# A fused linear-attention and two-layer kernel: dummy matmuls ahead of the first turning, the diagonals of two stages and the sums of three states moved off TensorE, and a redrawn head

## The chip, the cores and the metric

The kernel runs on one core of a Trainium2 chip. The metric is device microseconds (us) of one execution, the median of several runs. The core's engines each work through a stream of their own, in order: PE (TensorE, matmuls into the accumulators, eight banks called ps), DVE (VectorE), ACT (ScalarE), POOL (GpSimd, which here also issues the loads) and SP (which issues DMA transposes and the stores). Engines wait for each other on semaphores alone.

## What is computed

```python
state = zeros(B, H, D, D)                 # B, H, S, D = 4, 8, 768, 48
for t in range(S):
    cur = einsum('bhd,bhe->bhde', u * k[:, :, t], v[:, :, t])
    y[:, :, t] = einsum('bhd,bhde->bhe', r[:, :, t], state + cur)
    state = w[:, :, None] * state + einsum('bhd,bhe->bhde', k[:, :, t], v[:, :, t])
x = y.transpose(0, 2, 1, 3).reshape(3072, 384)
h = x @ w_in                              # 384 x 2048
out = maximum(0.01 * h, h) @ w_out        # 2048 x 384
```

Inputs and output are fp32; the kernel works in bf16 with fp32 accumulation.

## The kernel before

The 4 x 768 tokens are cut into 24 stages of 128 tokens, six to a batch element (`n % 6`). The recurrence is done stage by stage: inside a stage as a masked 128 x 128 product of decayed r and k, between stages by a state of 48 x 48 per head. Two stages make a pair `m` of 256 tokens for the two layers. Each step of a stage is a function, and a string of tokens, ORDER (L26 to L31), says in which order the steps of stages 0 to 9 are recorded; after it a loop (L725) does the rest pair by pair. Recording order is the order of each engine's stream, so a step that must wait holds up everything recorded behind it on the same engine. The tokens, with the number of the stage:

- `P` prep: DVE multiplies r and k by tables of decay (L322 and L324, from stage 8 on both in one, L315). From stage 8 (TURNED) SP then transposes the product by DMA (L317).
- `T` turn: for stages 0 to 7, PE transposes r and k by eight matmuls against `ident` (L367), and ACT copies the two banks out (L378; one of stage 0's on DVE, L375).
- `A`: eight matmuls give the 128 x 128 products (L391, two banks). `M`: DVE multiplies each bank by the triangular `mask` and writes `at` (L409), or from stage DIAG on overwrites only the part under the mask (L401), since `at` then already holds the diagonal.
- The diagonal (u) term. Below DIAG: `X`, a DVE product (L329), four matmuls with N = 2 inside `K` (L421), `Q`, a DVE product with v (L337), and three matmuls against `ident` inside `Y` (L513). From DIAG on: `Q` is three DVE instructions (L342, L344, L346) and two POOL tiles (L354).
- `K`: PE forms k-transposed times v (L425), and for stages below DIAG with `n % 6 > 0` adds the old state by one matmul against `ident` (L430). `S`: DVE multiplies by the decay (L475); from DIAG on it adds the old state itself first (L478, L480).
- `Y`: PE makes the stage's output (L508), ACT copies it to `xT` (L528). `G n.g`: 12 matmuls of layer one for one stage and a quarter of w_in (L541) and ACT's leaky ReLU (L546). `J m.j`: six matmuls for an eighth of w_in and a whole pair (L558). `H n`: layer two, 16 matmuls with N = 384 (L575). From pair 8 on layer two is done by seven half-size products (L639).
- `C` and `W`: 24 matmuls of one row (L449, L450), ACT's logarithms (L457) and tables (L466), DVE casts (L459) for the decays. `U`: one matmul and one copy for u's table (L710, L712). `F n`: n dummy matmuls, 128 x 512, of a tile of ones into the bank that is next (L254); nothing reads them. Three are there: two (EARLY) ahead of the broadcast of w (L294), one from the token `F1`.

Loads are issued by POOL (L217 a stage's r, k or v; L227 a quarter of w_in; L231 a quarter of w_out), stages 1 to 7 and all weights in the order of the string LOADS (L25), then the `L` tokens, which wait for a matmul of layer one (`pace`). POOL also makes `ident` (L262) and `mask` (L266) in the midst of the loads.

The eight banks are given out in rotation (`next_bank`): a step that takes a bank waits for whoever reads what was there eight takings ago.

Of the kernel before, what the change touches and what calls it, by code (L numbers as in the profile page):

```python
# [20 lines left out]
NFB = DFF // 128  # L21
NSL = HD // 128

FIRST, EARLY = 6, 2
LOADS = """r1 k1 r2 k2 wi0 id v1 r3 tri k3 v2 wi1 k4 r4 v3 wi2 k5 r5 r6 k6 v4 v5 k7 wi3 r7 v6 v7 wo3 wo2 wo1 wo0"""  # L25
ORDER = """  # L26
C W P0 P1 F1 T0 T1 P2 A0 X0 M0 A1 K0 T2 Q0 X1 Y0 A2 S0 M1 K1 X2 G0.0 Q1 P3 S1 Y1 T3 K2 M2 G1.0 X3 A3 U G0.1 S2 G1.1 Q2 M3 Y2 K3 P4
T4 Q3 G2.0 G2.1 G0.2 S3 G2.2 G1.2 Y3 P5 A4 P6 X4 M4 T5 X5 G3.0 K4 Q4 A5 S4 T6 G3.1 K5 G3.2 Y4 M5 L8 Q5 Y5 P7 A6 G1.3 J2.0 J2.1 T7
M6 X6 X7 K6 J2.2 J2.3 A7 S6 J2.4 J2.5 L9 Q6 G2.3 G0.3 J2.6 M7 L10 J2.7 L11 G3.3 K7 S7 P8 Q7 Q8 P9 H0 Q9 K8 H1 P10 L12 K9 H2 S8 S9
Y6 Y7 A8 A9 P11 M8 H3 M9 L13  # L30
"""  # L31


# [87 lines left out]
def bass_rwkv5_eagle__then__act_leaky_relu_kernel(  # L121
# [14 lines left out]
        return ctx.enter_context(nc.sbuf_tensor(name, shape, dt))  # L136

    NQK, NTP, NVS, NAT, NT, NX, NG, NO, NRK = 6, 6, 6, 6, 6, 3, 3, 4, 14
    TURNED, DIAG = 8, 8
    SEVEN = (8,9,10,11)  # L140
    HF, NH = NFB // 2, HD // 2
    w_in_sb = SB("w_in_sb", [128, NSL, DFF])
# [15 lines left out]
    tcol = SB("tcol", [128, 1], FP32)  # L158
# [7 lines left out]
    ones = SB("ones", [128, 512])  # L166
    mask = SB("mask", [128, 128])
    ident = SB("ident", [128, 128])
    ku = [SB(f"ku{i}", [128, HD]) for i in range(2)]
    rku = [SB(f"rku{i}", [128, HD]) for i in range(2)]  # L170
    s_tok = [SB(f"s_tok{i}", [128, H], FP32) for i in range(2)]
# [47 lines left out]
    def load_stage(n, pace=()):  # L219
        for which in "krv":  # L220
            load_one(n, which, pace)
# [12 lines left out]
    def row(h):  # L234
# [23 lines left out]

    ps_w, key_w = next_bank()

    def identity():
        add("pool", lambda: G.affine_select(ident[:, :], ones[:, 0:128], pattern=[[1, 128]], compare_op=ALU.is_equal,  # L262
                                            fill=0.0, base=0, channel_multiplier=-1), R=["ones"], W=["ident"])

    def triangle():
        add("pool", lambda: G.affine_select(mask[:, :], ones[:, 0:128], pattern=[[1, 128]], compare_op=ALU.is_ge,  # L266
                                            fill=0.0, base=-1, channel_multiplier=-1), R=["ones"], W=["mask"])

    for name in LOADS.split():
        if name == "id":  # L270
            identity()
        elif name == "tri":
            triangle()
        elif name[:2] == "wi":
            load_win(int(name[2:]))
        elif name[:2] == "wo":
            load_wout(int(name[2:]))
        else:
            load_one(int(name[1:]), name[0])

    add("dve", lambda: V.tensor_scalar(kexp[:, :], tcol[:, :], -1.0, float(MID - 1), ALU.mult, ALU.add),
        R=["tcol"], W=["kexp"])
    add("dve", lambda: V.tensor_scalar(qexp[:, :], tcol[:, :], 1.0, float(-MID), ALU.mult, ALU.add),
        R=["tcol"], W=["qexp"])
# [24 lines left out]

    def prep(n):  # L310
        iq = n % NQK
        if n >= TURNED:
            both = rk_sb[:, n % NRK, :, :].rearrange("p w (h d) -> p (w h) d", d=D)
            by = tab[:, :, :].rearrange("p w (h d) -> p (w h) d", d=D)
            add("dve", lambda: V.tensor_tensor(qk[iq][:, :, 0:D], both, by, ALU.mult),  # L315
                R=[("r", n % NRK), ("k", n % NRK), "qtab", "ktab", ("qk0", iq)], W=[("qp", iq), ("kp", iq)])
            add("sp", lambda: SP.dma_start_transpose(tp[n % NTP][:, :, :],  # L317
                                                     qk[iq][:, :, :].rearrange("p h e -> p (h e)")),
                R=[("kp", iq), ("qp", iq), ("qk0", iq)], W=[("tp", n % NTP, 0), ("tp", n % NTP, 1)],
                dma=f"tp{n % NTP}")  # L320
            return
        add("dve", lambda: V.tensor_tensor(qk[iq][:, 0:H, 0:D], hd(r_of(n)), hd(qtab[:, :]), ALU.mult),  # L322
            R=[("r", n % NRK), "qtab", ("qk0", iq)], W=[("qp", iq)])
        add("dve", lambda: V.tensor_tensor(qk[iq][:, H:2 * H, 0:D], hd(k_of(n)), hd(ktab[:, :]), ALU.mult),  # L324
            R=[("k", n % NRK), "ktab", ("qk0", iq)], W=[("kp", iq)])
# [33 lines left out]
    def turn(n):  # L359
        it, iq = n % NTP, n % NQK  # L360
        for half in ((0, 1) if n == 0 else (1, 0)):
            ps_t, key = next_bank()

            def emit(half=half, ps_t=ps_t):
                for p in range(NP):
                    h0 = half * H + 2 * p
                    last = PE.matmul(ps_t[:, 128 * p:128 * p + 128],  # L367
                                     qk[iq][:, h0:h0 + 2, :].rearrange("p h e -> p (h e)"), ident[:, :],
                                     start=True, stop=True)
                return last  # L370

            add("pe", emit, R=[("kp" if half else "qp", iq), ("qk0", iq), "ident"], W=[key])
            dst = tp[it][:, NP * half:NP * half + NP, :].rearrange("p m t -> p (m t)")
            if n == 0 and half == 1:
                add("dve", lambda dst=dst, ps_t=ps_t: V.tensor_copy(dst, ps_t[:, :]),  # L375
                    R=[key], W=[("tp", it, half)])
            else:
                add("act", lambda dst=dst, ps_t=ps_t: A.activation(dst, ps_t[:, :], AF.Copy),  # L378
                    R=[key], W=[("tp", it, half)])

    def a_mm(n):
        it = n % NTP
# [11 lines left out]

        add("pe", emit, R=[("tp", it, 0), ("tp", it, 1)], W=[key for _, key in at_bank[n]])

    def a_mask(n):
        if n >= DIAG:
            i = at_bank[n][0][1][1]
            halves = [("at", n % NAT, hh) for hh in range(2)]  # L400
            add("dve", lambda: V.copy_predicated(  # L401
                at[n % NAT][:, :, :, :].rearrange("p two m i -> p (two m) i"),
                mask[:, :].bitcast(mybir.dt.uint16).unsqueeze(1).to_broadcast([128, H, 128]),
                ps_all[:, 512 * i:512 * i + 1024].rearrange("p (m i) -> p m i", i=128)),
                R=[key for _, key in at_bank[n]] + ["mask"] + halves, W=halves)
            return
        for hh in range(2):
            part = at_bank[n][hh][0][:, :].rearrange("p (m i) -> p m i", i=128)
            add("dve", lambda hh=hh, part=part: V.tensor_tensor(  # L409
                at[n % NAT][:, hh, :, :], part, mask[:, :].unsqueeze(1).to_broadcast([128, NP, 128]), ALU.mult),  # L410
                R=[at_bank[n][hh][1], "mask"], W=[("at", n % NAT, hh)])

    def kv_mm(n):
        iq = n % NQK
        ps_kv, key = kv_bank[n] = next_bank()
        live, carried = n % NC < NC - 1, n < DIAG and n % NC > 0

        def emit():
            if n < DIAG:
# [288 lines left out]
    def u_table():  # L708
# [3 lines left out]
        add("act", lambda: A.activation(u_tab[:, :], ps_u[:, 0:HD], AF.Copy), R=[key], W=["u_tab"])  # L712

    steps = {"U": u_table, "P": prep, "Q": prep2, "T": turn, "A": a_mm, "M": a_mask, "K": kv_mm, "S": state, "Y": y_part, "X": diag, "C": decay_columns, "W": decay_table, "F": fill,
             "G": g1, "J": g1_pair, "H": g2, "L": lambda n: load_stage(n, pace=[("pace", (n - 4) // 2, (n - 4) % 2)])}
# [9 lines left out]
    for m in range(FIRST // 2, NST // 2):  # L725
# [92 lines left out]
```

## Time and profile before

| | us |
|---|---|
| three runs | 170.43, 170.77, 171.89 (median 170.77) |
| the profiled execution | 171.27 |
| its span, first to last instruction | 169.5 |
| busy PE, DVE, POOL, ACT | 163.1, 114.9, 103.8, 93.3 |
| first matmul of `T0` | 7.30 from the span's start |
| end of ORDER, first matmul of the loop | 54.96 |

Times inside the profile count from the span's start. A busy PE is one that has a matmul in flight. A line of the chain of waits shows a start, a length, the engine, the tile and the line of code. In a line of a group, the last number before the second bar is the mean length of one instruction in ns.

### The profile page before, as it was taken

The page shows a single profiled execution, that of the slowest core. Times are in us where ns is not written, and L with a number is a line of the kernel's source. Part 1 is how long each engine was busy: PE and PEld are TensorE (multiplying, and loading weights), DVE is VectorE, ACT ScalarE, POOL GpSimd, SP SyncE. Part 2 cuts the span into 40 slices and gives each one's busy share as a digit, 9 for nine tenths or more (in the row PEclk, how much of TensorE's full clock was granted, in tenths as well). Part 3 has the DMA queues.
Part 4 walks back from the last instruction along what each step waited for, and adds up shares of the span by engine and source line. Part 5 has one row for each costly group of instructions (what it writes and reads, how often), then busy time and mean ns, then how long its engine had stood idle before and what let it go on. Part 6 is the DMA issues. An engine that isn't in the chain of part 4 may idle for free.

```text
span 169.5 us, 5112 instructions
## 1 busy us (share of the span) xinstructions
PE 163.1 (96%) x2203; PEld 129.1 (76%) x2203; DVE 114.9 (68%) x211; ACT 93.3 (55%) x176; POOL 103.8 (61%) x117
## 2 busy tenths in 40 slices
PE   6799999999999999999999999999999999999992
PEld 1577898889656876876866867867867899898991
DVE  7699766752998869379289299099199976053272
ACT  4752888789122852842933934824834836829320
POOL 7999999990379799791992995974506500000000
PEclk9999999999999999999999999999999999999999
DMA  5999999999999989999699499599107102011032
GB/s 95 117 155 159 170 155 171 194 185 145 126 167 197 167 50 126 214 73 114 172 74 156 130 74 154 135 106 205 51 0 173 48 4 93 4 40 55 4 115 70
DMA packets 99258, 19.66 MB, mean 116 GB/s; under 512 B 92322, under 2 KB 99236, under 8 KB 99236
## 3 DMA queue, kind: packets, MB, share of 16 engines
q0 software_dynamic: 76512, 10.03, 90.9%
q1 hardware_dynamic: 21682, 9.11, 25.6%
q8 instruction: 17, 0.28, 0.7%
q10 hardware_dynamic: 1042, 0.20, 0.6%
q14 instruction: 5, 0.04, 0.1%
HBM read 20.45 MB, written 4.72 MB: 148 GB/s over the span
## 4 chain that ended last, share of the span: by engine, by line
PE 93%; POOL 4%; ACT 1%; issue 1%; DVE 0%; DVEq 0%; POOLq 0%
PE ps_all L558 31%; PE ps_all L575 25%; PE ps_all L639 11%; PE ps_all L541 7%; PE ps_all L508 7%; PE ps_all L391 4%; PE ps_all L367 3%; PE ps_all L425 3%; POOL rk_sb L217 2%; PE ps_all L513 1%; ACT tp L378 1%; POOL v_sb L217 1%; PE ps_all L430 1%; PE ps_all L421 1%; POOL w_in_sb L227 0%
## 5 line engine op out<-in xcount | busy, mean ns | idle before, releaser
L558 PE MATMUL ps_all<-xT,w_in_sb 128*128 128x256 bf16 x480 | 54.5, 273 | 0.0
L354 POOL TENSOR_TENSOR at<-ident,s_tok 128x512 bf16<-128x512 bf16 x32 | 35.0, 1121 | 29.0 <-DVE s_tok L346 29.0
L558 PEld LDWEIGHTS ps_all<-xT,w_in_sb 128*128 128x128 bf16 x480 | 46.7, 98 | 6.1
L564 ACT ACTIVATE gT<-ps_all 128x512 bf16<-128x512 f32 x80 | 47.7, 597 | 5.8 <-PE ps_all L558 1.2
L575 PE MATMUL ps_all<-w_out_sb,gT 128*128 128x384 bf16 x256 | 43.3, 326 | 0.0
L575 PEld LDWEIGHTS ps_all<-w_out_sb,gT 128*128 128x128 bf16 x256 | 24.4, 98 | 15.9
L401 DVE CAST_PREDICATED at<-mask,ps_all 128x1024 bf16<-128x1024 uint16 x16 | 18.8, 1219 | 20.6 <-PE ps_all L391 20.6
L581 ACT ACTIVATE out_sb<-ps_all 128x384 f32<-128x384 f32 x16 | 7.8, 490 | 38.4 <-PE ps_all L575 38.4
L217 POOL DMA_DIRECT2D v_sb<-in_v_dram x24 | 22.6, 945 | 0.4 <-issue 0.4
L217 POOL DMA_DIRECT2D rk_sb<-in_k_dram x23 | 21.6, 941 | 0.0
L217 POOL DMA_DIRECT2D rk_sb<-in_r_dram x23 | 21.3, 929 | 0.0
L670 DVE TENSOR_TENSOR out_sb<-ps_all,snap 128x192 f32<-128x192 f32 x13 | 4.4, 355 | 15.1 <-PE ps_all L639 14.5
L344 DVE TENSOR_TENSOR rku<-rk_sb,ku 128x384 bf16<-128x384 bf16 x16 | 13.8, 861 | 0.6
L528 ACT ACTIVATE xT<-ps_all 128x384 bf16<-128x384 f32 x24 | 11.0, 490 | 5.1 <-PE ps_all L508 3.0
L541 PE MATMUL ps_all<-xT,w_in_sb 128*128 128x128 bf16 x192 | 13.0, 225 | 0.0
L541 PEld LDWEIGHTS ps_all<-xT,w_in_sb 128*128 128x128 bf16 x192 | 11.8, 101 | 0.5 <-issue 0.3
L409 DVE TENSOR_TENSOR at<-ps_all,mask 128x512 bf16<-128x512 f32 x16 | 10.2, 682 | 2.2 <-PE ps_all L391 2.2
L546 ACT ACTIVATE gT<-ps_all 128x512 bf16<-128x512 f32 x16 | 9.6, 599 | 3.8 <-PE ps_all L541 3.1
L508 PE MATMUL ps_all<-at,v_sb 128*32 128x128 bf16 x384 | 11.4, 228 | 0.0
L378 ACT ACTIVATE tp<-ps_all 128x512 bf16<-128x512 f32 x15 | 8.2, 596 | 3.7 <-PE ps_all L367 3.7
L508 PEld LDWEIGHTS ps_all<-at,v_sb 128*32 128x32 bf16 x384 | 8.4, 99 | 2.2 <-issue 0.5
L508 PE MATMUL ps_all<-tp,st 128*32 128x128 bf16 x240 | 9.8, 223 | 0.0
(80 smaller groups left out, 197.2 us busy)
## 6 DMA issues: line engine op xcount, KB each, us to landing
out_dram<-out_sb SPq DMA_DIRECT2D x22, 192.0 KB, 2.6
v_sb<-in_v_dram POOLq DMA_DIRECT2D x24, 96.0 KB, 5.5
rk_sb<-in_r_dram POOLq DMA_DIRECT2D x23, 96.0 KB, 5.2
rk_sb<-in_k_dram POOLq DMA_DIRECT2D x23, 96.0 KB, 4.6
w_in_sb<-in_moe_w_in_dram POOLq DMA_DIRECT2D x4, 384.0 KB, 7.0
w_out_sb<-in_moe_w_out_dram POOLq DMA_DIRECT2D x4, 384.0 KB, 10.9
out_dram<-out_sb SPq DMA_DIRECT2D x4, 96.0 KB, 1.7
tp<-qk SPq DMA_TRANSPOSE x16, 4.4
```

The costliest lines, as they stand in the source:

```text
L217: add("pool", lambda: G.dma_start(dst, src), R=pace, W=[key], dma=f"{which}{n}")
L344: add("dve", lambda: V.tensor_tensor(rku[i2][:, :], r_of(n), ku[i2][:, :], ALU.mult), R=[("r", n % NRK), ("ku", i2)], W=[("rku", i2)])
L354: add("pool", lambda hh=hh, s_of=s_of: G.tensor_tensor(at[ia][:, hh, :, :], ident[:, :].unsqueeze(1).to_broadcast([128, NP, 128]), s_of.un ...
L401: add("dve", lambda: V.copy_predicated(at[n % NAT][:, :, :, :].rearrange("p two m i -> p (two m) i"), mask[:, :].bitcast(mybir.dt.uint16). ...
L409: add("dve", lambda hh=hh, part=part: V.tensor_tensor(at[n % NAT][:, hh, :, :], part, mask[:, :].unsqueeze(1).to_broadcast([128, NP, 128]) ...
L508: last = PE.matmul(ps_y[32 * q:32 * q + 32, 128 * s:128 * s + 128], a, m, start=first_mm and (s == 0 or n >= DIAG), stop=last_mm and n >= ...
L528: add("act", lambda: A.activation(xT[m % NX][:, :, 128 * half:128 * half + 128], ps_y[:, 0:HD].rearrange("p (s t) -> p s t", t=128), AF.Copy),
L541: last = PE.matmul(ps_g[:, 128 * f:128 * f + 128], w_in_sb[:, s, 128 * fb:128 * fb + 128], xT[ix][:, s, t], start=s == 0, stop=s == NSL - 1)
L558: last = PE.matmul(ps_g[:, 256 * f:256 * f + 256], w_in_sb[:, s, 128 * fb:128 * fb + 128], xT[ix][:, s, :], start=s == 0, stop=s == NSL - 1)
L564: add("act", lambda: A.activation(gT[ig][:, 2 * j:2 * j + 2, :].rearrange("p f t -> p (f t)"), ps_g[:, :], AF.Prelu, alpha=0.01), R=[key], ...
L575: last = PE.matmul(ps_o[:, 0:HD], gT[ig][:, s, 128 * half:128 * half + 128], w_out_sb[:, s, :], start=s == 0, stop=s == NFB - 1)
L639: done = PE.matmul(ps_o[:, 0:NH], lhs[:, s, :], rhs[:, s, :], start=first and s == 0, stop=s == HF - 1, skip_group_check=not (first and last))
```

## The change

Seven things, in one diff:

1. Dummies: EARLY 3, and ORDER holds `F5` between `P0` and `T0`, `F2` behind `C`, `F2` behind `P1`, `F1` behind `T1`. `C` moves behind `T0`.
2. DIAG 6: stages 6 and 7 take the diagonal from POOL tiles.
3. CARRY 3: only stages 1 and 2 add the old state on PE; 3, 4 and 7 on DVE.
4. A POOL ramp of 128 x 128 (column minus row) replaces the column `tcol`; DVE derives the two exponents, `ident` and `mask` from it.
5. `M n.how`: bits of `how` name halves that ACT first copies out of the bank, for DVE to multiply in place in SBUF (`M0.1`, `M3.3`).
6. Prep as one instruction from stage 4 on; both copies of `T0` on ACT.
7. ORDER holds the loads too (lower-case tokens), and all is in another order: stage 3 ahead of stage 2, `wi2` the first quarter of w_in, `v6` and `v7` behind all of w_out and the loads of stages 8 and 9. `L n` loads two stages.

```diff
-FIRST, EARLY = 6, 2
-LOADS = """r1 k1 r2 k2 wi0 id v1 r3 tri k3 v2 wi1 k4 r4 v3 wi2 k5 r5 r6 k6 v4 v5 k7 wi3 r7 v6 v7 wo3 wo2 wo1 wo0"""
+FIRST, EARLY = 6, 3
 ORDER = """
-C W P0 P1 F1 T0 T1 P2 A0 X0 M0 A1 K0 T2 Q0 X1 Y0 A2 S0 M1 K1 X2 G0.0 Q1 P3 S1 Y1 T3 K2 M2 G1.0 X3 A3 U G0.1 S2 G1.1 Q2 M3 Y2 K3 P4
-T4 Q3 G2.0 G2.1 G0.2 S3 G2.2 G1.2 Y3 P5 A4 P6 X4 M4 T5 X5 G3.0 K4 Q4 A5 S4 T6 G3.1 K5 G3.2 Y4 M5 L8 Q5 Y5 P7 A6 G1.3 J2.0 J2.1 T7
-M6 X6 X7 K6 J2.2 J2.3 A7 S6 J2.4 J2.5 L9 Q6 G2.3 G0.3 J2.6 M7 L10 J2.7 L11 G3.3 K7 S7 P8 Q7 Q8 P9 H0 Q9 K8 H1 P10 L12 K9 H2 S8 S9
-Y6 Y7 A8 A9 P11 M8 H3 M9 L13
+P0 r3 r1 k1 F5 T0 C F2 W X0 k3 U wi2 P1 F2 A0 r2 k2 v1 P3 K0 M0.1 S0 T1 F1 Q0 T3 A1 X1 Y0 P2 T2 K1 M1.0 k4 r4 v2 A3 X3 Q1 X2 v3 S1 P4 M3.3 G0.2 A2 Y1 M2 K2 T4 S2 wi0 K3 Q3 G1.2 Q2 G0.0 S3 G1.0 Y3 A4 k6 k5 v4 r5 r6 P5 wi3 Y2 X4 G3.2 v5 wi1 K4 P6 k7 T5 M4.0 Q4 r7 S4 G2.0 G2.2 G0.3 G3.3 A5 Y4 X5 T6 M5 K5 G2.3 Q5 G2.1 Y5 wo3 wo0 wo2 wo1 G0.1 G3.1 L8 P7 v7 T7 v6 J2.7 J2.0 Q6 Q7 J2.5 G3.0 J2.4 A6 M6 L10 A7 M7 J2.3 J2.1 P8 Q8 P9 G1.3 G1.1 H2 H0 K6 J2.2 K7 K9 J2.6 Q9 K8 S6 H3 S7 S8 A8 Y6 P11 S9 P10 Y7 A9 M8 L12 H1 M9
 """
...
-    TURNED, DIAG = 8, 8
+    TURNED, DIAG, CARRY = 8, 6, 3
...
-    add("pool", lambda: G.iota(tcol[:, :], pattern=[[0, 1]], base=0, channel_multiplier=1,
-                               allow_small_or_imprecise_dtypes=True), W=["tcol"])
+    add("pool", lambda: G.iota(ramp[:, :], pattern=[[1, 128]], base=0, channel_multiplier=-1,
+                               allow_small_or_imprecise_dtypes=True), W=["ramp"])
     load_one(0, "v")
+    add("dve", lambda: V.memset(ones[:, :], 1.0), W=["ones"])
     add("dve", lambda: V.memset(one_row[:, :], 1.0), W=["one_row"])
-    add("dve", lambda: V.memset(ones[:, :], 1.0), W=["ones"])
...
-    def identity():
-        add("pool", lambda: G.affine_select(ident[:, :], ones[:, 0:128], pattern=[[1, 128]], compare_op=ALU.is_equal,
-                                            fill=0.0, base=0, channel_multiplier=-1), R=["ones"], W=["ident"])
-
-    def triangle():
...
+    add("dve", lambda: V.tensor_scalar(ident[:, :], ramp[:, :], 0.0, None, ALU.is_equal), R=["ramp"], W=["ident"])
...
+    add("dve", lambda: V.tensor_scalar(mask[:, :], ramp[:, :], 1.0, None, ALU.is_ge), R=["ramp"], W=["mask"])
...
-        if n >= TURNED:
+        if n >= 4:
...
+            if n >= TURNED:
+                add("sp", lambda: SP.dma_start_transpose(tp[n % NTP][:, :, :],
...
-            if n == 0 and half == 1:
-                add("dve", lambda dst=dst, ps_t=ps_t: V.tensor_copy(dst, ps_t[:, :]),
-                    R=[key], W=[("tp", it, half)])
-            else:
-                add("act", lambda dst=dst, ps_t=ps_t: A.activation(dst, ps_t[:, :], AF.Copy),
-                    R=[key], W=[("tp", it, half)])
+            add("act", lambda dst=dst, ps_t=ps_t: A.activation(dst, ps_t[:, :], AF.Copy),
+                R=[key], W=[("tp", it, half)])
...
-    def a_mask(n):
+    def a_mask(n, how=0):
...
+            if (how >> hh) & 1:
+                raw, half = at[n % NAT][:, hh, :, :], ("at", n % NAT, hh)
+                add("act", lambda raw=raw, part=part: A.activation(raw, part, AF.Copy),
+                    R=[at_bank[n][hh][1]], W=[half])
+                add("dve", lambda raw=raw: V.tensor_tensor(
+                    raw, raw, mask[:, :].unsqueeze(1).to_broadcast([128, NP, 128]), ALU.mult),
+                    R=["mask", half], W=[half])
+                continue
...
-        live, carried = n % NC < NC - 1, n < DIAG and n % NC > 0
+        live, carried = n % NC < NC - 1, n < CARRY and n % NC > 0
...
-        if n % NC == 0 or n < DIAG:
+        if n % NC == 0 or n < CARRY:
...
+        if name[0].islower():
+            load(name)
+            continue
...
-        for n in (2 * m + 8, 2 * m + 9):
-            if n < NST:
-                load_stage(n, pace=[("pace", 2 * m, 0)])
-        for n in ahead:
-            if n < DIAG:
-                diag(n)
+        if 2 * m + 8 < NST:
+            load_pair(2 * m + 8, pace=[("pace", 2 * m, 0)])
```

More of the change, by code (lines that the diff above doesn't have):

```diff
@@ L157, in bass_rwkv5_eagle__then__act_leaky_relu_kernel @@
     qtab, ktab = tab[:, 0, :], tab[:, 1, :]
-    tcol = SB("tcol", [128, 1], FP32)
     qexp = SB("qexp", [128, 1], FP32)
@@ L168, in bass_rwkv5_eagle__then__act_leaky_relu_kernel @@
     ident = SB("ident", [128, 128])
+    ramp = SB("ramp", [128, 128], FP32)
     ku = [SB(f"ku{i}", [128, HD]) for i in range(2)]
@@ L217, in load_one, with load_two, load_pair @@
         add("pool", lambda: G.dma_start(dst, src), R=pace, W=[key], dma=f"{which}{n}")
-    def load_stage(n, pace=()):
-        for which in "krv":
-            load_one(n, which, pace)
+    def load_two(n, which, pace=()):
+        load_one(n, which, pace)
+        load_one(n + 1, which, pace)
+    def load_pair(n, pace=()):
+        for i in (n, n + 1):
+            for which in "krv":
+                load_one(i, which, pace)
     win_view = moe_w_in.rearrange("(s p) f -> p s f", p=128)
@@ L259, in bass_rwkv5_eagle__then__act_leaky_relu_kernel, with load @@
     ps_w, key_w = next_bank()
-    def identity():
-        add("pool", lambda: G.affine_select(ident[:, :], ones[:, 0:128], pattern=[[1, 128]], compare_op=ALU.is_equal,
-                                            fill=0.0, base=0, channel_multiplier=-1), R=["ones"], W=["ident"])
-    def triangle():
[L266 to L274, printed above, removed]
+    def load(name):
+        if name[:2] == "wi":
             load_win(int(name[2:]))
@@ L277, in bass_rwkv5_eagle__then__act_leaky_relu_kernel @@
             load_wout(int(name[2:]))
+        elif name[:2] in ("rr", "kk", "vv"):
+            load_two(int(name[2:]), name[0])
         else:
             load_one(int(name[1:]), name[0])
[L281 to L284, printed above, removed]
+    add("dve", lambda: V.tensor_scalar(kexp[:, :], ramp[:, 0:1], 1.0, float(MID - 1), ALU.mult, ALU.add),
+        R=["ramp"], W=["kexp"])
+    add("dve", lambda: V.tensor_scalar(qexp[:, :], ramp[:, 0:1], -1.0, float(-MID), ALU.mult, ALU.add),
+        R=["ramp"], W=["qexp"])
+    add("dve", lambda: V.tensor_scalar(ident[:, :], ramp[:, :], 0.0, None, ALU.is_equal), R=["ramp"], W=["ident"])
     add("dve", lambda: V.memset(v_sb[:, :, :].rearrange("p n (h e) -> p (n h) e", e=E)[:, :, D:E], 0.0), W=["v0"])
@@ L316, in prep @@
                 R=[("r", n % NRK), ("k", n % NRK), "qtab", "ktab", ("qk0", iq)], W=[("qp", iq), ("kp", iq)])
[L317 to L320, printed above, removed]
+            if n >= TURNED:
+                add("sp", lambda: SP.dma_start_transpose(tp[n % NTP][:, :, :],
+                                                         qk[iq][:, :, :].rearrange("p h e -> p (h e)")),
+                    R=[("kp", iq), ("qp", iq), ("qk0", iq)], W=[("tp", n % NTP, 0), ("tp", n % NTP, 1)],
+                    dma=f"tp{n % NTP}")
             return
@@ L714, in bass_rwkv5_eagle__then__act_leaky_relu_kernel @@
     steps = {"U": u_table, "P": prep, "Q": prep2, "T": turn, "A": a_mm, "M": a_mask, "K": kv_mm, "S": state, "Y": y_part, "X": diag, "C": decay_columns, "W": decay_table, "F": fill,
-             "G": g1, "J": g1_pair, "H": g2, "L": lambda n: load_stage(n, pace=[("pace", (n - 4) // 2, (n - 4) % 2)])}
+             "G": g1, "J": g1_pair, "H": g2, "L": lambda n: load_pair(n, pace=[("pace", (n - 4) // 2, (n - 4) % 2)])}
     for name in ORDER.split():
+        if name[0].islower():
+            load(name)
+            continue
         steps[name[0]](*(int(x) for x in name[1:].split(".") if x))
```

## The prediction

> **What bounds the kernel now.** I read the page's busy shares first, then the chain of waits in order of time, then the stretches of the head, then DVE's timeline and the loads.
>
> The page: PE is in work for nearly the whole span.
>
> ```profile
> PE 163.1 (96%) x2203; PEld 129.1 (76%) x2203; DVE 114.9 (68%) x211; ACT 93.3 (55%) x176; POOL 103.8 (61%) x117
> ```
>
> The chain, cut to the head (start, length, what):
>
> ```profile
> 7.30 1.57 PE ps_all L367 x12
> ...
> 10.04 0.61 PE ps_all L391 x6
> ...
> 14.42 1.28 PE ps_all L541 x12
> ...
> 17.53 0.16 PE ps_all L430
> 17.70 0.67 PE ps_all L541 x12
> ...
> 21.36 0.08 PE ps_all L421 x4
> ...
> 26.09 0.27 PE ps_all L513 x3
> 26.36 0.33 PE ps_all L391 x8
> ...
> 54.96 5.13 PE ps_all L558 x47
> ```
>
> Two things are to be seen. From about 16.5 us on PE steps follow each other without a hole, so a PE instruction taken out there shortens the run by its pitch. Before that PE is at half speed: 12 matmuls of L541 take 1.28 at 14.42 and 0.67 at 17.70. The granted clock's column shows 1.00 for the head too; the pitch says otherwise, and I go by the pitch. At full pitch the work done from 7.30 to 16.65 (T0 to T2, A0 to A2, K0, K1, Y0, Y1, G0.0) would take 4.9; it took 9.35. So the head gives away 4.4 there, and 7.3 ahead of it.
>
> Is it PE that sets the head's pace? The stretches (busy PE, PEld, DVE, ACT, POOL) say that DVE is as full:
>
> ```profile
> 7.30:16.65 9.35, 9.14 (x127) 6.91 (x128) 8.73 (x21) 3.85 (x7) 9.35 (x12) 1.00 1.82 150
> 16.65:22.80 6.15, 6.05 (x127) 5.35 (x124) 4.62 (x10) 4.99 (x10) 6.15 (x8) 1.00 2.20 164
> ```
>
> DVE has work in 8.73 of the first 9.35, so a faster PE meets a busy DVE. Third, the loads:
>
> ```profile
> 9.52 0.36 DVE L324 TENSOR_TENSOR qk<-rk_sb,tab 128x384 bf16<-128x384 bf16 x1 [0.19 <-DMA rk_sb<-in_k_dram]
> ...
> 23.30 0.36 DVE L322 TENSOR_TENSOR qk<-rk_sb,tab 128x384 bf16<-128x384 bf16 x1 [0.45 <-DMA rk_sb<-in_r_dram]
> ...
> 44.00 0.36 DVE L344 TENSOR_TENSOR rku<-rk_sb,ku 128x384 bf16<-128x384 bf16 x1
> ...
> 56.04 2.23 DVE L344 TENSOR_TENSOR rku<-rk_sb,ku 128x384 bf16<-128x384 bf16 x1
> ```
>
> DVE waits for landings, not for POOL's issue. With issue plus time to landing, the fifth load (k2, issued 5.07) lands at 9.5, wi0 at 11.9, r7 (22.15) at 30.1, v7 (23.93) at 32.0, the last w_out quarter (27.00) at 39.8: about 0.70 for a stage's r, k or v and 1.95 for a weight, back to back. The last two lines, for later: L344 takes 0.36 alone and 2.23 beside a POOL tile.
>
> **The change, part by part.**
>
> *PE work taken out.* Three L430 at 0.16 are 0.48; L421 in stages 6 and 7, 2 x 0.08; L513, 2 x 0.27 as at 26.09 (2 x 0.18 where nothing waits on its end). Together 1.2 (1.0 at the least), all on the dense PE. What pays: DVE needs L478 and L480 (0.59 + 0.41 in pitch) for L475 (0.47), 0.5 more for each of states 3, 4 and 7; the cover is DVE's wait for r5 (0.45 above) and its idle 2.07 and 3.37 at 36 to 42. Stages 6 and 7 get L342, L344, L346 (0.39 + 0.39 + 0.47 in pitch) for L329 and L337 (0.8): 0.45 more each, and 2.2 of POOL tiles each. POOL has 6.69 idle ahead of 45.03, so they fit. If that cover is gone, M7 waits, behind it P8's transposes, and then A8.
>
> *ident and mask.* T0 waited 1.0 for POOL's ident (end 7.25). On DVE from a ramp no row shows it; L409's 128x512 in 0.68 gives 0.17 by size, its whole 0.68 the upper end, a gain excluded since it is added work. I take 0.2 each, hidden: DVE idles 1.27 ahead of 6.16, and that wait goes since P0 now stands ahead of the casts. The wider iota costs POOL between 0.0 and 0.44 (0.13 now, L262's 0.57 at most); POOL is rid of L262 and L266, 1.0.
>
> *T0's start.* The third early dummy (0.43) pushes L294 by 0.1. The first table is ready at 5.6; L322 0.56 gives 6.2. F5 from 4.3 at 0.43 ends at 6.4. T0 starts at 6.4 instead of 7.30: 0.9.
>
> *T0 to A0.* Both copies on ACT: tp0 is ready at 8.2, not 9.1. But PE's stream has C (1.48 at half speed), F2, U and F2 between. At full speed, taking C at 0.9, that is 0.9 + 0.43 + 0.2 + 0.43, and A0 begins at 9.2, as before (9.21). At half speed it is 3.5, and A0 begins at 10.8. This is where dummies cost. I take full speed from about 8: in the old head it came right behind the first 3.5 us without a hole (12.95 to 16.5), and the new list has no hole from 4.3 on.
>
> [...]
>
> *M0 to K4.* DVE's stream at row pitches: casts 8.8, X0 9.1, P1 9.7, P3 10.2 (k3 is now the fifth load, 9.6), M0's masked half from SBUF (0.34 as L329, same size; upper end 0.60 as L409) and direct half 11.4 (before 11.4), S0, Q0 12.3, X1, then P2. Its k2 is now the eighth load, behind wi2: lands 13.5. So T2 goes at 14.0 (before 10.99), PE waits about 1.0 there. M1 15.2, Q1, X2, S1, P4 17.2, M3's halves 17.9 (saving 0.26 each), M2 19.1, S2, Q3, Q2, S3 21.5. PE: Y1 16.2, K2 16.9, T4 17.3, G0.0 at 19.6 (wi0 follows v3's 17.0 by 2.0 to 3.1), Y3 20.9, Y2, G3.2, K4 23.3, T5 23.6. The work ahead of T5 is smaller by G's and larger by T's and A's than before's.
>
> *T5 to the end of ORDER.* From here every wait is covered by my landings (wi3 25.1, wi1 27.8, r7 29.2 to 30.1). The list up to H2 is T5, T6, T7 (0.45), eleven G (0.67), six J (0.655), A5 to A7 (0.33), Y4, Y5 (0.70), K5: 15.1, so H2 at 38.7, plus 0.5 for small waits such as the 0.10 of issue at 18.37: 39.2. H2 needs the last w_out, 39.8 less two loads moved behind it: 38.4. After two H (2.60 each) K6 at 44.4 needs v6, eight loads later: 44.0. Then 8.7 of work (H3 and H1 5.2, A8, A9, Y6, Y7 1.5, the rest J and K): the end at 53.1 instead of 54.96. SP: P11's transposes now go ahead of P10's, at about 51; they took 4.4 in the median, A10 comes at 58.3, so about 2 are left.
>
> *Sum.* 54.96 - 53.1 = 1.8: 0.9 from T0, 1.2 from PE work, 0.3 lost to dummies and loads. Nothing behind it changes: the loop and the tail are dense in both. From the profiled execution 171.27 - 1.8 = 169.5; that execution stands 0.5 above the median 170.77, so against the median 169.0.
>
> **The rivals.**
>
> *The loads are quicker.* The floor is K6 at 44.0, hence 52.7 and 168.6. The old list lost 1.2 more at wi1 (17.9, 3.1 after v2) than at other weights; if that does not recur, v6 is there at 42.8 and the end at 51.5: 167.4. For it: landings are the only limit in the late head. Against: DVE must be 1.2 earlier too. 0.15.
>
> *The clock stays low through the dummies.* For it: 4.6 us of matmuls in flight did not open it before. Then A0 goes at 10.8, T2 at 15.3, Y1 at 18.3, but wi0, r5 and wi3 land when they land, and T5 is late by about 0.9: gain 0.9, 169.9. 0.22.
>
> *The other side.* Same place, but nothing behind it hides the delay: DVE's in-order list (M0, S0, Q0, M1, M2, Q2) shifts by A0's 1.6, and every Y waits on it; U and F1 at half speed add 0.5. 1.6 + 0.5 - 1.2 = 0.9 lost: 171.7, or 172.6 if T0 gains nothing. It decides where A0 begins: after 10.5 with Y3 after 22. For it: DVE full in the head. Against: DVE sheds M halves, T0's cast and L324's (0.15 a stage). 0.16.
>
> **How the numbers follow.** My case has 0.47, own range 168.3 to 169.9; with the rivals 0.15, 0.22 and 0.16. The range runs from the quick loads' 167.4 to the other side's 171.7. A per cent is 1.7, about what a measurement can tell from no change. Faster by more: two thirds of my case (169.0 is just beyond the mark of 169.06) plus the quick loads, 0.46. Slower by more than 172.5: half of the other side, and some for what I did not see, 0.11. Within: 0.43.
>
> **What would show it.** T0's first matmul near 6.4, with no wait for ident. A0's eight matmuls in 0.33 (fast) or 0.54 (slow), at 9.2 or 10.8. T2 waiting for DVE's P2 and that for k2. H2 at about 39 and K6 at 44 with a wait for v6. L430 three fewer, L421 24, L513 18. The loop's first L558 at 53. I would be wrong if PE is dense well before T5, if DVE waits for POOL tiles at M6 or M7, or if A10 waits for a transpose.

## The result and the profile after

The changed kernel takes 172.84 us (median of four runs, 171.61 to 173.88) against 170.8 before: 1.0102 times, 95% interval 1.0055 to 1.0149. It is slower by 1%, where 169.0 was forecast, and outside the range. Ratios here and below leave out executions that took over 1.5% more than the fastest of the same kernel. The profiled execution took 171.61, with a span of 169.8; it is the fastest of the four, 1.2 below the median, so what it shows is not the whole loss.

The page's first part. Against before, PE is busy 1.6 us less, and DVE 1.4 less. The PE work did go: of the matmuls that were L430, L421 and L513, 2, 24 and 18 are left of 5, 32 and 24.

```profile
PE 161.5 (95%) x2195; PEld 126.7 (75%) x2196; DVE 113.5 (67%) x211; ACT 95.2 (56%) x180; POOL 106.6 (63%) x119
```

The chain of waits up to the loop (start, length, what), cut to the places that the prediction named:

```profile
6.74 0.85 PE ps_all L361 x8
...
8.80 0.54 PE ps_all L255 x2
9.34 0.26 PE ps_all L708
9.60 0.54 PE ps_all L255 x2
10.14 0.35 PE ps_all L381 x8
...
23.55 0.45 PE ps_all L361 x8
23.99 0.22 PE ps_all L539 x4
24.22 0.61 issue
24.82 2.62 PE ps_all L539 x44
...
30.43 0.22 PE ps_all L506 x7
30.66 0.64 issue
...
40.45 5.20 PE ps_all L573 x32
45.65 0.17 PE ps_all L423 x4
...
52.63 7.82 DMA tp<-qk
60.45 0.14 issue
60.59 0.62 PE ps_all L381 x16
```

Lines are those of the changed kernel: L361 turns, L381 is `A`, L255 the dummies, L539 `G`, L573 `H`, L506 `Y`. A piece of the chain begins where the one before it ends; the first matmuls themselves start a little earlier (T0 at 6.53, A0 at 10.07, T5 at 23.38, H2 at 40.29, K6 at 45.49, the loop's first L556 at 54.17). Four things are to be seen. T0 does start 0.8 earlier than before. Between it and A0 stand two dummies, U, two dummies. Twice, inside one step, PE stops with nothing to wait for ("issue"). And the chain goes through a DMA transpose that took 7.82 from its issue: that is A10 waiting, once, for 1.0 us. PE's waits say the same (who waits for whom: us in total, times, the longest):

```profile
PE ps_all L381 <- DMA tp<-qk: 1.0, 1, 1.0
PE ps_all L506 <- issue: 0.6, 1, 0.6
...
PE ps_all L539 <- issue: 0.6, 1, 0.6
```

SP's timeline shows one reason why that transpose was late (L581 is a store, L311 a transpose). P11's product was ready at 49.28 and its transpose was issued at 51.17, behind three stores of which the last is H3's, whose matmuls end at 50.18; these hold SP from 44.65 to 51.13.

```profile
44.65 6.48 SPq L581 DMA_DIRECT2D out_dram<-out_sb  x3
51.17 5.03 SPq L311 DMA_TRANSPOSE tp<-qk  x2
```

Before, the same two transposes were issued at 48.72 and 51.42 and landed at 52.80 and 57.87. Now they landed at 58.94 and 60.45. So there is a second reason: they took 7.8 us each from issue to landing, where before they took 4.1 and 6.5.

**The arithmetic of the miss.** The prediction's sum gave 171.27 - 1.8 = 169.5 for a profiled execution; it took 171.61, 2.14 more. The end of ORDER, the loop's first matmul, came at 54.17 for 53.1: 1.07. The loop's first J stretch (48 matmuls, up to A10) took 6.41, with A10's wait at its end, where it took 5.34 before: 1.07. The small rest: the 54.96 that the table ahead of the prediction gives for the loop's first matmul is where the chain's piece begins, and the trace has that matmul at 54.80, so the base was 0.16 too late; and what follows A10 took 0.17 less than before. On top of this comes 1.7 up to the median: the median stands 1.2 above the profiled execution, where it was taken to stand 0.5 below. The second profile of the same kernel, next, bears on that.

### The profile page after: what moved, and what is told of

Read it like the earlier page. It is cut to its first block, busy times and chain, and to the rows that moved or that the text cites. A ratio compares the mean times of both kernels' runs of the same rounds, so it can differ in the third digit from the quotient of the medians.

```text
span 169.8 us, 5111 instructions
## 1 busy us (share of the span) xinstructions
PE 161.5 (95%) x2195; PEld 126.7 (75%) x2196; DVE 113.5 (67%) x211; ACT 95.2 (56%) x180; POOL 106.6 (63%) x119
## 4 chain that ended last, share of the span: by engine, by line
PE 83%; DVE 8%; DMA 5%; issue 2%; ACT 1%; DVEq 0%
PE ps_all L556 27%; PE ps_all L573 22%; PE ps_all L637 11%; PE ps_all L539 6%; PE ps_all L506 5%; DMA tp<-qk 5%; PE ps_all L381 3%; PE ps_all L255 3%; PE ps_all L423 2%; DVE at L407 2%; PE ps_all L361 1%; DVE at L391 1%; DVE sum_t L476 1%; PE ps_all L287 1%; DVE qk L308 1%
## 5 line engine op out<-in xcount | busy, mean ns | idle before, releaser
L348 POOL TENSOR_TENSOR at<-ident,s_tok 128x512 bf16<-128x512 bf16 x36 | 38.5, 1104 | 25.9 <-DVE s_tok L340 25.9
L556 PE MATMUL ps_all<-xT,w_in_sb 128*128 128x256 bf16 x480 | 54.7, 273 | 0.0
L556 PEld LDWEIGHTS ps_all<-xT,w_in_sb 128*128 128x128 bf16 x480 | 46.6, 98 | 6.1
L573 PE MATMUL ps_all<-w_out_sb,gT 128*128 128x384 bf16 x256 | 43.1, 326 | 0.0
L391 DVE CAST_PREDICATED at<-mask,ps_all 128x1024 bf16<-128x1024 uint16 x18 | 21.2, 1220 | 28.2 <-PE ps_all L381 28.1
L573 PEld LDWEIGHTS ps_all<-w_out_sb,gT 128*128 128x128 bf16 x256 | 24.4, 98 | 15.9
L213 POOL DMA_DIRECT2D v_sb<-in_v_dram x24 | 22.0, 926 | 0.3 <-issue 0.3
L213 POOL DMA_DIRECT2D rk_sb<-in_r_dram x23 | 20.8, 909 | 0.0
L668 DVE TENSOR_TENSOR out_sb<-ps_all,snap 128x192 f32<-128x192 f32 x13 | 4.5, 356 | 15.1 <-PE ps_all L637 14.5
L539 PE MATMUL ps_all<-xT,w_in_sb 128*128 128x128 bf16 x192 | 12.3, 219 | 0.6 <-issue 0.6
L338 DVE TENSOR_TENSOR rku<-rk_sb,ku 128x384 bf16<-128x384 bf16 x18 | 12.2, 679 | 0.6
L539 PEld LDWEIGHTS ps_all<-xT,w_in_sb 128*128 128x128 bf16 x192 | 11.1, 98 | 1.0 <-issue 0.7
L506 PE MATMUL ps_all<-at,v_sb 128*32 128x128 bf16 x384 | 10.9, 221 | 0.6 <-DVE vs L331 0.6
L308 DVE TENSOR_TENSOR qk<-rk_sb,tab 128x768 bf16<-128x768 bf16 x20 | 10.5, 552 | 0.5 <-DMA rk_sb<-in_r_dram 0.5
L506 PEld LDWEIGHTS ps_all<-at,v_sb 128*32 128x32 bf16 x384 | 8.1, 96 | 3.2 <-issue 1.0
L340 DVE TENSOR_REDUCE s_tok<-rku 128x8 f32<-128x384 bf16 x18 | 10.0, 553 | 0.6
L506 PE MATMUL ps_all<-tp,st 128*32 128x128 bf16 x240 | 9.7, 219 | 0.6 <-issue 0.6
```

The source lines that it names most:

```text
L338: add("dve", lambda: V.tensor_tensor(rku[i2][:, :], r_of(n), ku[i2][:, :], ALU.mult), R=[("r", n % NRK), ("ku", i2)], W=[("rku", i2)])
L348: add("pool", lambda hh=hh, s_of=s_of: G.tensor_tensor(at[ia][:, hh, :, :], ident[:, :].unsqueeze(1).to_broadcast([128, NP, 128]), s_of.un ...
L391: add("dve", lambda: V.copy_predicated(at[n % NAT][:, :, :, :].rearrange("p two m i -> p (two m) i"), mask[:, :].bitcast(mybir.dt.uint16). ...
L506: last = PE.matmul(ps_y[32 * q:32 * q + 32, 128 * s:128 * s + 128], a, m, start=first_mm and (s == 0 or n >= DIAG), stop=last_mm and n >= ...
L539: last = PE.matmul(ps_g[:, 128 * f:128 * f + 128], w_in_sb[:, s, 128 * fb:128 * fb + 128], xT[ix][:, s, t], start=s == 0, stop=s == NSL - 1)
L556: last = PE.matmul(ps_g[:, 256 * f:256 * f + 256], w_in_sb[:, s, 128 * fb:128 * fb + 128], xT[ix][:, s, :], start=s == 0, stop=s == NSL - 1)
```

## The experiments

All ratios are against the kernel before, run on the same chip. One per cent is 1.7 us.

**The changed kernel again** (no edit).

> The changed kernel once more, for its spread (171.6 to 173.9 so far, the profiled execution the fastest) and a second profile. Turning theory (the DMA transposes of stages 10 and 11 land late and A10 waits, 1.0 us in the first profile, more in slower executions): a slower profile shows a longer wait of A10 and the same head. Clock theory (the clock opens at another moment in each execution, 8.3 us in the first profile): a slower profile shows matmuls at half pitch beyond 10 us and the same wait of A10. Median about 172.5 by both.

Measured 173.13 (171.11 to 174.24, ten runs), 1.0105 (1.0070 to 1.0140). This profile has a span of 171.5, 1.7 more than the first, and one difference comes first: the clock. The granted clock's column stands at 1.00 until its first record. When PE became fast is told by the pitch, the time from one matmul's start to the next one's, and by the start of that record: 8.3 us in the first profile and 16.7 in this one. PE's timeline of this profile (start, length, line), for the four pieces from L255 to L381 in the first one's chain above:

```profile
8.99 1.03 PE L255 MATMUL ps_all<-ones 128*128 128x512 bf16 x2
9.96 0.50 PE L708 MATMUL ps_all<-u_row,one_row 1*128 1x384 bf16 x1
10.39 1.03 PE L255 MATMUL ps_all<-ones 128*128 128x512 bf16 x2
11.36 0.61 PE L381 MATMUL ps_all<-tp 48*128 48x128 bf16 x8
```

From C's end to A0, the dummies and U take 1.34 us in the first execution (8.73 to 10.07) and 2.37 in this one (8.99 to 11.36). A0 starts 1.3 later, T5 2.0 later (25.40), the loop 1.3 later (55.45), and A10's wait grows to 1.4, so each of the two theories has a part of the 1.7. Of the five profiles of kernels with all these dummies, three have the clock open at 7.3 to 8.3 and two at 16.6 to 16.7. The times suggest that an early clock is the rarer in executions without a profile: two of these ten are within 0.3 of the first profile's 171.61 or under it, the others at 172.9 or more.

**Transposes earlier.**

```diff
-K8 S6 H3 S7 S8 A8 Y6 P11 S9 P10 Y7 A9
+K8 S6 P10 P11 H3 S7 S8 A8 Y6 S9 Y7 A9
```

> The changed kernel with the preparations and transposes of stages 10 and 11 ahead of layer two of stage 3, so that SP does not hold them behind that store. Turning theory: A10 waits for nothing, and the median falls by 1.2 to 2.5, to 170 to 171.3, and the spread becomes that of the kernel before. Clock theory: 1.2 at the most, and the spread stays over 2 us.

Measured 172.06, 1.0046 (1.0023 to 1.0070), 0.6% less than the kernel unchanged. The transposes are issued at 47.51 and 48.83, land at 52.32 and 54.84, A10 no longer waits, and the J stretch is back at 5.34 (PE's timeline, A10 without a wait):

```profile
60.07 0.62 PE L381 MATMUL ps_all<-tp 48*128 48x128 bf16 x16
```

So the second half of the miss, 1 us, is shown. The gain is under the 1.2 to 2.5 of the turning theory, as the clock theory said; the spread, 1.5 but for one execution of 174.30, is no wider than that of the kernel before (2.0 on this chip), as the turning theory said. So here too each has a part.

**Few dummies.**

```diff
-FIRST, EARLY = 6, 3
+FIRST, EARLY = 6, 2
...
-P0 r3 r1 k1 F5 T0 C F2 W X0 k3 U wi2 P1 F2 A0
+P0 r3 r1 k1 F1 T0 C W X0 k3 U wi2 P1 A0
...
-S0 T1 F1 Q0 T3
+S0 T1 Q0 T3
```

> The changed kernel with the dummies of the kernel before (two, and one ahead of the first turning). If the dummies pay, the clock opens later, about 13 to 16 us, and the time is 1 to 2 us above the changed kernel's. If they only stand in PE's way (F2, U and F2 take 1.34 between the first turning and A0 even at full speed), the time is the same or up to 0.8 us less, since DVE and the loads set the pace of the head.

Measured 171.34, 1.0023 (0.9997 to 1.0050): 0.8% less than with them, 1.4 us, more than the 0.8 that was expected at the most. Here the clock opens at 15.5, so the head runs at half speed up to there, and yet the head is no later: T5 starts at 23.57, against 23.38 in the first profile with its clock open from 8.3. DVE's timelines say why (start, length, line; L407 is `M`, here M0's second half, and L308 is P4). The changed kernel's, first profile:

```profile
11.60 0.69 DVE L407 TENSOR_TENSOR at<-ps_all,mask 128x512 bf16<-128x512 f32 x1
...
16.80 0.55 DVE L308 TENSOR_TENSOR qk<-rk_sb,tab 128x768 bf16<-128x768 bf16 x1
```

And that of the kernel with few dummies:

```profile
11.21 0.69 DVE L407 TENSOR_TENSOR at<-ps_all,mask 128x512 bf16<-128x512 f32 x1
...
16.85 0.55 DVE L308 TENSOR_TENSOR qk<-rk_sb,tab 128x768 bf16<-128x768 bf16 x1
```

A0 is 1.15 earlier at half speed, M0 0.4 earlier, and P4 on DVE stands where it stood. With DVE's list in order and nearly full (8.86 busy of the 9.40 between 14.10 and 23.50 in the changed kernel), the early clock of the first profile bought PE nothing by T5. That is shown for a head with dummies ahead of A0 alone: no run had an early clock without them.

**Only the work off PE, in the old order.**

```diff
-    TURNED, DIAG = 8, 8
+    TURNED, DIAG, CARRY = 8, 6, 3
...
-Y5 P7 A6 G1.3 J2.0 J2.1 T7 M6 X6 X7 K6 J2.2 J2.3 A7 S6 J2.4 J2.5 L9 Q6 G2.3
+Y5 P7 Q6 A6 G1.3 J2.0 J2.1 T7 M6 K6 J2.2 J2.3 Q7 A7 S6 J2.4 J2.5 L9 G2.3
```

with `carried` and the state's test on `CARRY`, as in the change.

> The kernel before with only DIAG 6 and CARRY 3, its order kept but for the two stages' POOL tiles made ahead of their masks. If a matmul taken out of the dense stretch shortens the run by its pitch, 1.0 to 1.2 us less than the kernel before (169.6 to 169.8). If the removed work is lost to waits on DVE or POOL, no change or slower.

Measured 173.28, 1.0135 (1.0090 to 1.0180): slower by 2.3 us, though PE does less. The gain became waits. PE's timeline (of this kernel, with the lines of before):

```profile
35.66 1.48 PE L558 MATMUL ps_all<-xT,w_in_sb 128*128 128x256 bf16 x12 [1.29 <-DVE at L401]
...
52.59 0.40 PE L391 MATMUL ps_all<-tp 48*128 48x128 bf16 x8 [1.01 <-DMA tp<-qk]
```

And DVE's, where L401 is the mask and L354 POOL's tile:

```profile
39.01 1.22 DVE L401 CAST_PREDICATED at<-mask,ps_all 128x1024 bf16<-128x1024 uint16 x1 [1.70 <-POOL at L354]
```

PE's first wait is for M6's mask on DVE, which starts at 34.38, right behind POOL's tile (end 34.34) and K6 (34.37). M7's mask waits 1.70 for POOL's tile. And A9 waits for P9's transpose. The prediction had named a chain of this kind for the case that its cover is gone, "M7 waits, behind it P8's transposes, and then A8". Its first link is there in the old order and not in the new one; the others are not: P8's transpose landed at 49.68, for 49.84 before, and P9's was issued only 0.2 later than before (45.64) but took 6.8 us for 5.4. Why it took longer is open, and so is how much of the 2.3 comes from where the POOL tiles were put in the old order.

**Only the states on DVE, in the old order** (`CARRY` 3, `DIAG` 8).

> The kernel before with CARRY 3 alone: three matmuls of 0.16 less on PE, three additions more on DVE. By PE's pitch 0.5 us less than the kernel before; if DVE's 0.5 more for each state delays the steps behind it, no change or up to 1 us more. With the diagonals of stages 6 and 7 taken along the same kernel was 2.0 us above the kernel before, so this tells which of the two costs.

Measured 171.35, 1.0019 (0.9996 to 1.0041): no gain from 0.48 of PE work removed. So most of the loss above came with the diagonals.

**Each of the two put back in the new order**, with few dummies: `CARRY` 8, and `DIAG` 8 with X6 X7 where Q6 Q7 stood and Q6 Q7 behind K7.

> The changed kernel with few dummies and the states of stages 3, 4 and 7 added on PE again (CARRY 8). By PE's pitch 0.5 us more than few dummies alone. If that gain was lost to DVE's added 0.5 for each state, as in the old order, the same or less.

Measured 172.12, 1.0059 (1.0030 to 1.0089): 0.4% above few dummies, 0.6 us, but the intervals overlap. Its profile shows two waits of 1.2 that few dummies alone hasn't: one for the late transposes, and one of K3, whose matmul now needs the state that DVE's S2 writes (19.19 to 19.74; K3 starts at 19.83). So what shows is a wait, not the PE work's own length.

> The changed kernel with few dummies and the diagonals of stages 6 and 7 on PE again (DIAG 8, the DVE products in the place of the three DVE instructions and the POOL tiles). By PE's pitch 0.7 us more than few dummies alone. If the POOL tiles are what makes the loads of stages 10 and 11 late (issued 4.1 later, r11 landing at 47.9 to 49.9), the loads land earlier and it is the same or up to 1 us less.

Measured 173.02, 1.0134 (1.0091 to 1.0176), 1.9 us above few dummies, far more than the PE work alone. PE waits 0.9 for ACT in an `A` and 0.4 for a quarter of w_in in this profile, which few dummies alone doesn't; the order wasn't redrawn for it. These two and the 0.7 of PE work would make 2.0. The other theory is out: without the POOL tiles r11 was still issued at 40.49 and landed at 49.28 (40.27 and 48.96 with few dummies alone). So the diagonals off PE seem to pay in the new order, by about their pitch as an estimate; the rest is a misfit of the order. The states are not shown to pay.

**Y5 behind the last two G.** Where a kernel with the new order stops without a releaser, it does so at the same two places of PE's stream: near the 692nd and the 944th matmul or weight load. Of the twelve profiles with that order eight have both stops, three only the second (few dummies, the states put back, and "states first" below), and the first joining, below, has none. In the changed kernel they are 0.83 us at 24.00 and 0.86 at 30.44, start to start. The trace's instruction queue (q8) brings a packet of 16,384 B shortly ahead of each, from 22.45 to 23.34 and from 28.80 to 29.70; PE goes on 1.5 to 1.6 us after a packet's end. The kernel before passes the two counts 2.6 and 1.8 us after the packets' ends, and doesn't stop. That PE lacks its next instructions there is my estimate from these times; no run shows it. By it, a step of short matmuls comes to the same count sooner and waits longer, so Y5 (28 quick matmuls, 0.50 in all) was moved away from it:

```diff
-G2.1 Y5 wo3 wo0 wo2 wo1 G0.1 G3.1 L8
+G2.1 wo3 wo0 wo2 wo1 G0.1 G3.1 Y5 L8
```

> The changed kernel with the output of stage 5 behind two layer-one steps, nothing else. Instruction theory (PE runs out of instructions there; the next block is there at about 31.3 us in three kernels whatever they do): the same instruction number passes at 31.3 again, with less or no hole ahead of it, as 48 longer instructions stand in for 48 of the shorter ones: 0.3 to 0.8 us less than the changed kernel. Rival (the output of stage 5 waits for DVE): the hole goes away altogether, since DVE was done at 29.7.

Measured 172.48, 1.0073 (1.0042 to 1.0105), 0.3% less than unchanged, but the intervals overlap. The second stop takes 0.42, where it took 0.86 in the first profile of the unchanged kernel; but in the second one, whose clock opened as late as here (16.6), it took 0.60, and the first stop 0.35 where it takes 0.62 here. So the trace shows no gain. The rival is out, since a stop at 944 remains. The same edit with the best order (below) gives 0.2%, within the intervals too.

**More instructions ahead of it in the old order**: 32 matmuls of 128 x 2 behind the dummy F1, so that the same count comes earlier.

> The kernel before with 32 tiny matmuls (128 x 2, 64 more instructions) in the 1.0 us in which PE waits for ident. Instruction theory: they take no PE time that was used, but push 64 instructions of work behind the block's border that passes at about 31.4; a hole of 0.5 to 1.8 us opens there and the run is longer by as much. Rival (instructions are free as long as PE idles): no change, 0.1 at the most.

Measured 171.75, 1.0033 (1.0003 to 1.0063), 0.6 us more, but not by a hole: there is no stop at 944, which passed at 30.04; the packet too came earlier (landed at 28.14). So neither theory came out, the packet does not come at a fixed time, and more instructions alone make no stop. Before, the packet's transfer begins about 2.9 us after the previous such place in the stream is passed; in the changed kernel 4.0. Why it is later there stays open: the page shows the DMA engines nine tenths busy or more then, but no run took loads away.

**First joining**: few dummies, transposes earlier and Y5 later, all at once.

> The changed kernel with few dummies, the preparations of stages 10 and 11 ahead of layer two of stage 3, and the output of stage 5 behind the two layer-one steps that followed it. If the losses are the dummies, the late transposes and PE's stream of instructions (a hole at one place of the stream, near instruction 944, that no engine explains), they add up: 170.0 to 170.6, below the kernel before. If the hole is a wait of the output of stage 5 for something else, 171 to 171.4 as with few dummies alone.

Measured 173.17 (170.81 to 175.84) against 171.08, where 170.0 to 170.6 was expected. Six of its twelve executions have a mean granted clock of 0.98 to 0.99 and take 173.4 or more; the ratio of the others is 1.0047 (1.0014 to 1.0080). The profile is of one of the six and shows why. The gains did not add up because P11, moved ahead, met its load: it waited 3.34 for r11, which landed at 49.78 (47.94 in the changed kernel). The states S7 to S9 stood behind it in DVE's list, and Y6 and Y7 behind those. DVE's timeline:

```profile
49.87 0.56 DVE L308 TENSOR_TENSOR qk<-rk_sb,tab 128x768 bf16<-128x768 bf16 x1 [3.34 <-DMA rk_sb<-in_r_dram]
```

PE's timeline, Y7 after its wait and then H1:

```profile
52.92 0.24 PE L506 MATMUL ps_all<-at,v_sb 128*32 128x128 bf16 x4 [1.56 <-DVE sum_t L476]
...
53.97 4.17 PE L573 MATMUL ps_all<-w_out_sb,gT 128*128 128x384 bf16 x16
```

Then the clock fell. The stretches (busy PE, PEld, DVE, ACT, POOL, granted clock, DMA share, GB/s):

```profile
50.00:53.40 3.40, 0.88 (x44) 0.63 (x44) 3.23 (x8) 0.49 (x1) 2.71 (x4) 1.00 1.86 130
53.45:56.85 3.40, 3.40 (x22) 1.65 (x19) 3.33 (x6) 0.49 (x1) 0.00 (x0) 0.50 1.72 180
```

PE had 0.88 of work in the first 3.40, and the granted clock was 0.50 in the next 3.40: H1 took 4.01 instead of the 2.61 of the changed kernel. So the clock fell here behind a stretch in which PE was not wholly idle.

**States first, then the transposes.**

```diff
-K8 S6 H3 S7 S8 A8 Y6 P11 S9 P10 Y7 A9
+K8 S6 S7 S8 S9 P10 P11 H3 A8 Y6 Y7 A9
```

> The changed kernel with few dummies, and with the states of stages 6 to 9 and then the preparations of stages 10 and 11 ahead of layer two of stage 3, so that neither DVE's states wait behind a load nor the transposes behind a store. If few dummies alone (1.0023 of the kernel before) still hold a wait of A10 in most executions, 0.3 to 1.0 us less than that: 170.2 to 171.0. If not, the same as few dummies alone.

With few dummies: 170.63 against 171.09, 0.9985 (0.9957 to 1.0013), as fast as before, and 0.4% under few dummies alone, within the range expected, though the two intervals overlap.

> The same with the output of stage 5 behind two layer-one steps. If the joined kernel lost only by DVE's wait of 3.3 for a load of stage 11 and the half clock behind it, that is gone here, and this is the fastest: 169.6 to 170.6, no execution above 172. If it lost because the loads of stages 8 to 11 can't be there for an earlier head, A8 to Y7 wait again and it is no faster than the one without that step.

The same with Y5 later: 170.13 (169.46 to 171.06) against 171.09, 0.9963 (0.9937 to 0.9989). This beats both kernels, the one before by 0.4%. Its chain from H1 on has no wait in it:

```profile
51.24 2.71 PE ps_all L573 x16
53.95 5.24 PE ps_all L556 x48
59.19 0.55 PE ps_all L381 x16
```

The margin is thin: the second transpose lands at 59.07, and A10's first matmul starts at 59.12.

**Dummies, put two ways into this best order**: only in PE's wait ahead of T0 (F4 for F1 there), and all of the change's.

> The best order so far (d2), with F4 in place of F1 ahead of T0: the dummies then lie only in PE's wait for the first preparation (their end is to be near 5.7, T0 started at 6.01 in d2), none between T0 and A0. Theory A, the dummies cost by their place in PE's way (F2, U, F2 ahead of A0): these are free, 169.8 to 170.6, as d2's 170.13. Theory B, dummies anywhere cost (by the clock that they spoil or the instructions that they add): 0.4 us or more above d2. If the clock's record opens near 8 in most executions, up to 0.5 us under d2.

> The same order with all dummies of the change (EARLY 3, F5, then F2, F2, F1 ahead of A0). Theory A: 1.0 to 1.8 us above d2 (171.1 to 171.9), A0 near 11.4 where the clock opens late, near 10.1 where it opens at 8. Rival: what the dummies cost in the change's own order was a matter of the late transposes, and with these gone the dummies cost under 0.5 (under 170.6).

Only in the wait: 170.4, 0.9960 (0.9936 to 0.9984); they are free, and buy nothing (clock open at 13.7, T5 at 23.43). All: 171.57, 1.0002 (0.9969 to 1.0034), 0.7 us more than this by the ratios and 1.2 by the medians. By the medians that is in the range of the theory that dummies cost by their place, by the ratios between it and the rival; the dummies' own price is thus about 1 us, and how much of the 1.4 that they cost in the change's order came through the late transposes is not shown. The times of this kernel fall into two groups, five of twelve at 169.9 to 170.3 and seven at 171.5 to 172.7. In its profile the clock opens at 7.3 and is lost again, at the wait ahead of T2 (stretches as above):

```profile
8.00:14.10 6.10, 4.64 (x78) 2.75 (x74) 4.80 (x15) 4.98 (x12) 6.10 (x8) 1.00 2.01 146
14.15:17.50 3.35, 3.29 (x35) 2.71 (x36) 3.00 (x8) 2.01 (x4) 3.35 (x5) 0.50 1.89 172
```

It was lost at 14.12, for 3.41 us. T5 starts at 24.73, 1.2 later than in the kernel with few dummies.

## Why the prediction was wrong

- *PE work taken out, 1.2.* Right that it is off PE and that POOL and DVE have the room in the new order (M6 and M7 wait for no POOL tile). Put back, the diagonals make the new order 1.1% slower, of which 1.3 us are waits; for the states nothing is shown.
- *ident and mask, hidden; T0 at 6.4.* Right: T0 at 6.53, `mask` 0.2 longer than taken but beside POOL's loads.
- *T0 to A0, at full speed, 9.2.* This step failed. In the profiled execution C ran mostly at half speed (1.21 for the 0.9 taken) and A0 came at 10.07; in the second one the clock stayed low to 16.7 and A0 came at 11.36. I took the kinder of two cases as the normal one, from one row of the old head. What decides between the two is not shown: of five profiles with these dummies three have the early clock and two the late one. Before, too, PE had matmuls in flight from 1.65 to 6.27, and T0 at 7.30 ran at 0.12 a matmul, where T3 at 16.65 took 0.056. The rival "the clock stays low" had the low clock, with A0 at 10.8, and the other side its consequence, DVE's list shifted behind A0 (Y3 at 22.67 in the second profile, after the 22 that it named); both were priced too low. Without the dummies ahead of it A0 comes at 8.92 with a late clock too.
- *M0 to K4.* Right in the first profile: T2 at 14.14 for 14.0, behind P2, T5 at 23.38 for 23.6. P2 did not wait for k2, as the text said it would: k2 had landed at 13.31, and DVE's list came to P2 at 13.46. In the second profile T5 came at 25.40. That DVE sets this stretch was in the text; that few dummies would then do just as well (23.57) was not drawn from it.
- *T5 to H2, 15.6.* This step failed too. It took 16.9. The two stops of 0.83 and 0.86 were in no row of before, and a term for them was missing; the 0.5 for small waits covered a part. (The listed work adds up to 15.3, not 15.1.) They are the 1.07 at the end of ORDER, which is whole by H2: 40.29 for 39.2, then 13.9 to the end as reckoned. Why PE stops there is open.
- *The loads.* H2 and K6 were said to be near their loads. The last w_out landed at 36.21 (for 38.4) and v6 at 41.82 (for 44.0): no wait. The rival "the loads are quicker" had that right, and it brought nothing, since PE was the limit.
- *SP: "A10 comes at 58.3, so about 2 are left".* This step failed too. The transposes took 7.8, not the 4.4 of the median, and A10 waited 1.0 to 1.4. The median was over all 16 of the run, of which the last two took 3.2 to 3.3; the four of this stretch took 4.1 to 6.5 before already. With the transposes issued earlier the wait is gone. The text did name this wait as what would prove it wrong.

Of the 2.14 by which the profiled execution missed the sum, then, about half is the stops and half the transpose. Of the 1.7 on top, 0.5 is the place that the sum gave the profiled execution against the median, and 1.2 fits the late clock: the profile that has it is 1.7 slower, 1.3 by the loop's start and 0.4 by A10's wait. No run held the clock fixed.

## What to carry to other kernels

Put dummy matmuls only where PE waits anyway: there they were free here (0.9960 of the kernel before, against 0.9963 without). On PE's way to the step that feeds the pacing engine they delayed it (with U, by 1.3 us here, and by 2.4 when the clock did not open). An early clock won nothing here by T5 (23.38, against 23.57 without it), where another in-order engine was nearly full (DVE, 8.86 of 9.40). Price a DMA transpose by those of the same stretch (4.1 to 6.5 us before) and not by the median of the run (4.4), and give its issue a place in its queue ahead of stores that wait for later work (A10's wait of 1.0 was gone then). PE work taken away was no gain in the old order (1.0135), where a mask then waited 1.70 for POOL's tile; take the same edit in the old order as the test.

## What the runs showed of the hardware

- The same kernel's PE clock opened at 8.31 us in one execution and at 16.71 in another, with dummies from 1.45 on in an almost unbroken stream. The record of full speed lasted 160.43 in the one and 153.60 in the other, and a half-speed record inside a run 3.41 (all dummies in the best order). In the 3.41 us ahead of the early opening PE had 2.7 us of matmuls of more than one row. In the other execution the stretches from 3.05 to 6.47 and from 6.47 to 9.88, which took in w's broadcast and C, held 2.0 each, and the one from 9.88 to 13.29 held 3.05; the clock opened behind none of the three. What opens it is not shown.
- The clock was lost behind 3.41 us that held 0.9 of PE work (first joining) and 1.9 (all dummies in the best order), and kept behind 2.3 (changed kernel, 11.72 to 15.14).
- PE stops of 0.35 to 1.26 us inside a burst, near the same two counts of its stream, 252 instructions apart, each ending 1.3 to 1.6 us after a 16,384 B packet of the instruction queue has landed. No run settled why the packet comes late.
- The same transpose of one stage landed 3.2 to 7.8 us after its issue in one execution of the changed kernel.
- A 128 x 384 product of DVE (L336) took 0.35 alone and 2.47 beside a POOL tile in the changed kernel, 2.93 in the first joining.
- The 128 x 128 ramp took POOL 0.23; DVE took 0.20 for `ident` and 0.40 for `mask`, which holds as much, where 0.2 had been taken for each.
